# Strassen's seven products in the last projection, for two pairs of token tiles

## The chip, the cores and the metric

The kernel runs on one core of one Trainium2 chip. A core has a matrix engine (TensorE, PE in the profile, whose weight loads are shown as PEld), three engines for elementwise work (VectorE or DVE, ScalarE or ACT, GpSimd or POOL), an engine that issues most transfers here (SyncE, SP), and 16 DMA engines. The metric is the device time of one execution in microseconds.

## The reference

Three layers follow each other on 1792 tokens (4 batches of 448) of 768 features.

```python
def _attn_ref(q, k, v, cap):             # 12 heads of 64
    scores = scale * np.matmul(q, k.transpose(0, 1, 3, 2))
    scores = cap * np.tanh(scores / cap)
    attn = np.exp(scores - max); attn = attn / (sum + 1e-09)
    return np.matmul(attn, v)
def _moe_ref(x, w_in, w_out):            # 768 -> 2048 -> 768
    h = x @ w_in
    return (h - np.tanh(h)) @ w_out
def _moe2_ref(x, w_in, w_out, g_ln):     # 768 -> 1024 -> 768
    h = x @ w_in
    solu = h * softmax(h)
    ln = (solu - mean) / np.sqrt(var + 1e-06) * g_ln
    return ln @ w_out
```

The change is in the last product, `ln @ w_out`, for tokens of the second half.

## The kernel before

The tokens are worked in two halves (`hb` 0 and 1) of 896 tokens, seven tiles of 128. Each half runs attention, then `moe1` (the MoE layer), then `moe2`. Inputs are 32-bit words of 64-bit floats. Each fp32 value that enters a product is split into a rounded high part and a low part (`h` and `l`), and a product is three matmuls (`mm3`, line 252): high by high, high by low, low by high. The split weights are spilled to DRAM in the first half (`keep`) and read back in the second (`unit`, line 178, into 13 rotating buffers of the pool `w`, on SP's queue).

In the second half the up-projection of `moe2` is already done by Strassen's seven products (`seven`, line 647); the sums of its weights are made and spilled in `moe1` by `sums_w3` (line 223), one call per chunk `c`, from spilled weights that are read back, and read as `T1` to `T4`.

Then each tile is normalised (`norm`, line 604): maximum on DVE, exponent with its sum on ACT, the product with `h`, statistics in two parts, root on POOL, scaling on DVE (line 625), eight PE transposes into PSUM (line 629), the high part `lh` by ACT (line 635), the low part `ll` by DVE (line 636). `project` (line 753) multiplies it: per contraction block of 128 six matmuls, three of 512 columns (`wide` weights) and three of 256 (`narrow`), into the two banks of one PSUM tile `oab`; ACT copies 512 columns into `ot`, DVE 256 (line 785), SP writes 128x768 out. The order of tiles is 0, 2, 4, 6, 1, 3, 5. The last tile does its wide part first (line 763).

The code outside attention is written in program order, and a scheduler of the language places each engine's instructions by its own costs, so neighbouring tiles interleave on PE, DVE and ACT. Each engine then runs its queue strictly in order. PSUM tiles of two banks come from two pools, `a` and `b`, of two tiles each; a tile is free again once everything that reads it has read it. The loop around the change is:

```python
for i, t in enumerate(order):
    if i + 1 < NTC:
        norm(order[i + 1])
    ...
    project(t)
```

Of the kernel before, what the change touches and what calls it, by code (L numbers as in the profile page):

```python
# [29 lines left out]
def fused_kernel(ctx, tc, qk_in, v, cap, w1, w2, w3, w4, gln, out):  # L30
    nc = tc.nc
    B, H, S, D = 4, 12, 448, 64
    DM = H * D
    P = 128
# [4 lines left out]
    NK = DM // P  # L39
    HB = B // 2  # L40
    HT = HB * S
    NTC = HT // P
# [25 lines left out]
    def pst(name, tag="b"):  # L68
        return psum[tag].tile([P, 2, 512], F32, tag=tag, name=name)
# [58 lines left out]
    saved = {}  # L128
# [70 lines left out]
    def cols(w, n):  # L199
        return [tuple(t[:, i * (512 // n):(i + 1) * (512 // n)] for t in w) for i in range(n)]  # L200
# [13 lines left out]
    def load_w4():  # L214
        g = [glt[:, i:i + 1] for i in range(DF2 // P)]
        wide, narrow = [], []
        for i in range(DF2 // P):
            wide.append(unit(f"4_{i}", w4u[i], 1, g[i:i + 1]))
            if i % 2:
                narrow += cols(unit(f"5_{i}", w4u[DF2 // P + i // 2], 2, g[i - 1:i + 1]), 2)  # L220
        return wide, narrow

    def sums_w3(i):

        def raw(j, kk):
            st = sp.tile([P, 2, 512], F32R, tag="st", name="rw", bufs=3)
            nc.sync.dma_start(st.bitcast(F32), saved[f"3_{j}_{kk}"].bitcast(F32))
            f = sp.tile([P, 512], F32, tag="f", name="fw", bufs=3)
            nc.vector.tensor_tensor(f, st[:, 0].bitcast(F32), st[:, 1].bitcast(F32), ALU.add)
            return f  # L230

        def put(p, f):
            w = sp.tile([P, 2, 512], F32R, tag="st", name="tw", bufs=3)
            nc.scalar.copy(w[:, 0], f)
            nc.vector.tensor_tensor(w[:, 1], f, w[:, 0].bitcast(F32), ALU.subtract)
            d = drw.tile([P, 2, 512], F32R, name=f"dT{p}_{i}")
            nc.sync.dma_start(d.bitcast(F32), w.bitcast(F32))
# [10 lines left out]
        b21 = raw(0, 2 * i + 1)  # L248
        nc.vector.tensor_tensor(b21, b21, t, ALU.subtract)
# [240 lines left out]
    def moe1(mp, hb, xh, xl, yh, yl):  # L490
# [95 lines left out]
        for c in range(NCHUNK):  # L586
            for k in range(2):
                if c + 1 < NCHUNK:
                    up(c + 1, k)
                if c:  # L590
                    down(c, range(k * NK // 2, (k + 1) * NK // 2))
            if c == 0:
                down(c)
            if hb and c < NK // 2:
                sums_w3(c)

    def moe2(mp, hb, yh, yl):
        hs = {}
        es = {}
        nk2 = DF2 // P  # L600
        lts = {}
        place.update(pool=(mp, WX2), at=-1)

        def norm(t):
            h = hs[t]
            mx = mp.tile([P, 1], F32, tag="mx", name="mx")
            if hb and t in order[1:3]:
                nc.vector.tensor_copy(mx, es[order[0]][:, :1])
            nc.vector.tensor_reduce(mx, h, AX.X, ALU.max)
            nc.vector.tensor_scalar(mx, mx, -1.0, None, ALU.mult)  # L610
            e = mp.tile([P, DF2], F32, tag="e", name="e")
            sm = mp.tile([P, 1], F32, tag="sm", name="sm")
# [8 lines left out]
            nc.vector.bn_aggr(mv, st)  # L621
            rstd = mp.tile([P, 1], F32, tag="rstd", name="rstd")
            nc.vector.tensor_scalar(rstd, mv[:, 1:2], 1e-6, None, ALU.add)
            nc.gpsimd.tensor_tensor(rstd, rstd, mhalf, ALU.pow)
            nc.vector.tensor_scalar(e, e, mv[:, 0:1], rstd, ALU.subtract, ALU.mult)
            es[t] = e
            tp = psum["a"].tile([P, nk2, P], F32, tag="a", name="tp")
            for kk in range(nk2):
                nc.tensor.transpose(tp[:, kk], e[:, kk * P:(kk + 1) * P], idf)
            if hb == 0 and t == order[-1]:  # L630
                lh, ll = (sp.tile([P, nk2, P], F32R, tag="st", name=m, bufs=3) for m in ("lhz", "llz"))
            else:
                lh = mp.tile([P, nk2, P], F32R, tag=f"lh{order.index(t) % 2}", name="lh", bufs=1)
                ll = mp.tile([P, nk2, P], F32R, tag=f"ll{order.index(t) % 2}", name="ll", bufs=1)
            nc.scalar.copy(lh, tp)
            nc.vector.tensor_tensor(ll, tp, lh.bitcast(F32), ALU.subtract)
            lts[t] = (lh, ll)

        groups = [list(range(t, min(t + 2, NTC))) for t in range(0, NTC, 2)]
        for gi, ts in enumerate(groups):  # L640
# [4 lines left out]
        order = list(range(NTC))  # L645
# [91 lines left out]
        if hb:  # L737
            order = list(range(0, NTC, 2)) + list(range(1, NTC, 2))
            seven()
        for j in range(0 if hb else 2):  # L740
            wt = load_w3(j)
            for gi, ts in enumerate(groups):
# [6 lines left out]
                if j == 1 and gi == NG:  # L749
                    norm(0)  # L750
        wide, narrow = load_w4()

        def project(t):
# [4 lines left out]
            ot = mp.tile([P, DM], F32, tag="ot", name="ot")  # L758
            if hb == 1 and t == order[-1]:
                ob = pst("ob", "a")[:, 0]  # L760

                for kk in range(nk2):
                    mm3(oa, (lh[:, kk], ll[:, kk]), wide[kk], kk == 0, kk == nk2 - 1)
                nc.scalar.copy(ot[:, 0:512], oa)
                nc.sync.dma_start(out[r0:r0 + P, 0:512], ot[:, 0:512])
                for kk in range(nk2):
                    mm3(ob[:, :256], (lh[:, kk], ll[:, kk]), narrow[kk], kk == 0, kk == nk2 - 1)
                nc.vector.tensor_copy(ot[:, 512:DM], ob[:, :256])
                nc.sync.dma_start(out[r0:r0 + P, 512:DM], ot[:, 512:DM])
                return  # L770
            for kk in range(nk2):
                f, l = kk == 0, kk == nk2 - 1
                sh, sl_ = lh[:, kk], ll[:, kk]
                (ah, al), (bh, bl) = wide[kk], narrow[kk]
                nc.tensor.matmul(oa, sh, ah, start=f, stop=False)  # L775
                nc.tensor.matmul(oa, sh, al, start=False, stop=False)  # L776
                nc.tensor.matmul(ob[:, :256], sh, bh, start=f, stop=False)
                nc.tensor.matmul(ob[:, :256], sh, bl, start=False, stop=False)
                nc.tensor.matmul(oa, sl_, ah, start=False, stop=l)  # L779
                nc.tensor.matmul(ob[:, :256], sl_, bh, start=False, stop=l)  # L780
            nc.scalar.copy(ot[:, 0:512], oa)
            if hb == 0 and t == NTC - 2:
                nc.scalar.copy(ot[:, 512:DM], ob[:, :256])
# [31 lines left out]
        for i, t in enumerate(order):  # L815
            if i + 1 < NTC:
                norm(order[i + 1])
            if hb == 0 and t == NTC - 1:
                return last()
            project(t)  # L820

    class Region:

# [21 lines left out]
    for hb in range(2):  # L845
# [4 lines left out]
        yh, yl = xtiles()  # L850
# [69 lines left out]
```

## Time and profile before

| | before |
|---|---|
| times of 3 runs, us | 893.17, 894.16, 895.63 (median 894.16) |
| profiled execution, us | 894.53 |
| its span, first to last instruction, us | 892.8 |
| PE, DVE, ACT busy, share of the span | 99%, 74%, 47% |
| moved by DMA | 160.27 MB, mean 180 GB/s |
| last projection, from its first whole run of matmuls | 824.4 to 889.5 us |

The span is what lies between the first and the last instruction of the program; the execution's time has a little around it. Starts in the rows are microseconds from the span's start. A matmul's duration overlaps the next one's, so the cost of one in a full stream is the distance between starts.

### The profile page before, as it was taken

The page shows a single profiled execution, that of the slowest core. Times are in us where ns is not written, and L with a number is a line of the kernel's source. Part 1 is how long each engine was busy: PE and PEld are TensorE (multiplying, and loading weights), DVE is VectorE, ACT ScalarE, POOL GpSimd, SP SyncE. Part 2 cuts the span into 40 slices and gives each one's busy share as a digit, 9 for nine tenths or more (in the row PEclk, how much of TensorE's full clock was granted, in tenths as well). Part 3 has the DMA queues.
Part 4 walks back from the last instruction along what each step waited for, and adds up shares of the span by engine and source line. Part 5 has one row for each costly group of instructions (what it writes and reads, how often), then busy time and mean ns, then how long its engine had stood idle before and what let it go on. Part 6 is the DMA issues. An engine that isn't in the chain of part 4 may idle for free.

```text
span 892.8 us, 13030 instructions
## 1 busy us (share of the span) xinstructions
PE 884.1 (99%) x5133; PEld 707.8 (79%) x5133; DVE 662.9 (74%) x999; ACT 422.3 (47%) x467; POOL 47.4 (5%) x88
## 2 busy tenths in 40 slices
PE   8999999999999999999999999999999999999998
PEld 4444699898898988888874457989989989887887
DVE  6687889989999991888347987894774644678951
ACT  7999367453453331443169990863532332212221
POOL 2211000000000000001012210000000000000000
PEclk9999999999999999999999999999999999999999
DMA  8554690697786774731155642358754332366101
GB/s 296 181 188 139 216 356 25 205 331 258 246 303 219 252 260 150 251 127 53 47 207 201 204 137 81 117 182 324 271 196 158 117 118 82 93 209 230 60 36 53
DMA packets 51177, 160.27 MB, mean 180 GB/s; under 512 B 10989, under 2 KB 14061, under 8 KB 51117
## 3 DMA queue, kind: packets, MB, share of 16 engines
q1 hardware_dynamic: 43932, 130.25, 42.6%
q0 software_dynamic: 7040, 29.20, 9.4%
q8 instruction: 40, 0.66, 0.3%
q14 instruction: 21, 0.16, 0.1%
q10 hardware_dynamic: 144, 0.00, 0.0%
HBM read 109.65 MB, written 49.62 MB: 178 GB/s over the span
## 4 chain that ended last, share of the span: by engine, by line
PE 81%; DVE 12%; DMA 3%; ACT 2%; issue 2%; POOL 0%; DVEq 0%; POOLq 0%; ACTq 0%
PE o L349 9%; PE op L571 6%; PE op L570 6%; PE op L569 6%; PE hp L510 6%; PE hp L511 6%; PE hp L512 6%; PE s L315 5%; PE hp L254 4%; PE hp L256 4%; PE hp L255 4%; PE oab L775 2%; PE oab L779 2%; PE oab L776 2%; PE x L321 2%; PE so L366 2%
## 5 line engine op out<-in xcount | busy, mean ns | idle before, releaser
L512 PE MATMUL hp<-xh,w 128*128 128x512 f32 (+2 forms) x384 | 139.7, 364 | 0.0
L511 PE MATMUL hp<-xl,w 128*128 128x512 f32 (+2 forms) x384 | 139.6, 363 | 0.0
L510 PE MATMUL hp<-xh,w 128*128 128x512 f32 (+2 forms) x384 | 139.4, 364 | 0.0
L569 PE MATMUL op<-gh,w 128*128 128x512 f32 (+1 forms) x336 | 122.0, 363 | 1.5 <-DVE acc L576 1.5
L571 PE MATMUL op<-gh,w 128*128 128x512 f32 (+1 forms) x336 | 122.2, 364 | 0.0
L570 PE MATMUL op<-gl,w 128*128 128x512 f32 (+1 forms) x336 | 122.1, 363 | 0.0
L510 PEld LDWEIGHTS hp<-xh,w 128*128 128x128 f32 x384 | 72.0, 188 | 9.4 <-issue 1.2
L511 PEld LDWEIGHTS hp<-xl,w 128*128 128x128 f32 x384 | 72.1, 188 | 8.0 <-issue 0.7
L512 PEld LDWEIGHTS hp<-xh,w 128*128 128x128 f32 x384 | 72.1, 188 | 7.9 <-issue 0.7
L349 PE MATMUL o<-t,vf 128*32 128x448 f32 x768 | 77.8, 542 | 0.0
L341 ACT ACTIVATE t<-t,shift,capt 128x3136 f32<-128x3136 f32 (+2 forms) x26 | 72.8, 2808 | 0.7
L569 PEld LDWEIGHTS op<-gh,w 128*128 128x128 f32 x336 | 63.1, 188 | 9.7 <-DVE acc L576 2.0
L570 PEld LDWEIGHTS op<-gl,w 128*128 128x128 f32 x336 | 63.0, 188 | 7.1
L571 PEld LDWEIGHTS op<-gh,w 128*128 128x128 f32 x336 | 63.0, 188 | 6.7
L538 ACT ACTIVATE u<-hp 128x896 f32<-128x896 f32 x32 | 29.5, 921 | 76.6 <-PE hp L512 76.6
L332 ACT ACTIVATE t<-s,tscale 128x1344 f32<-128x1344 f32 x48 | 63.5, 1379 | 2.1 <-PE s L315 2.1
L544 DVE SCALAR_TENSOR_TENSOR gf<-u,hp 128x896 f32<-128x896 f32 x32 | 34.7, 1084 | 33.1 <-ACT t L540 33.1
L119 ACT CAST w<-f 128x512 fp32r<-128x512 f32 x44 | 27.3, 623 | 66.8 <-DVE f L113 52.1
L349 PEld LDWEIGHTS o<-t,vf 128*32 128x32 f32 x768 | 22.7, 109 | 43.4 <-issue 38.7
L576 DVE TENSOR_TENSOR acc<-op,acc 128x896 f32<-128x896 f32 x36 | 39.1, 1086 | 21.9 <-PE op L571 21.9
L552 ACT CAST gh<-gf 128x896 fp32r<-128x896 f32 x32 | 29.8, 943 | 51.2 <-DVE gf L549 30.4
L113 DVE SCALAR_TENSOR_TENSOR f<-st,f 128x512 uint32<-128x512 uint32 x72 | 49.2, 688 | 1.0
(187 smaller groups left out, 1824.4 us busy)
## 6 DMA issues: line engine op xcount, KB each, us to landing
d<-w SPq DMA_DIRECT2D x69, 512.0 KB
w<-d SPq DMA_DIRECT2D x53, 512.0 KB
st<-in_moe_w_out_dram SPq DMA_DIRECT2D x35, 512.0 KB
st<-in_moe_w_in_dram SPq DMA_DIRECT2D x25, 512.0 KB
kq<-in_qk_dram POOLq DMA_DIRECT2D x21, 480.0 KB, 4.3
w<-d POOLq DMA_DIRECT2D x13, 512.0 KB, 5.3
rw<-d SPq DMA_DIRECT2D x12, 512.0 KB
dT<-tw SPq DMA_DIRECT2D x12, 512.0 KB
```

Source lines behind the costliest of these rows:

```text
L113: nc.vector.scalar_tensor_tensor(f, st[:, :, 0], 29, f, ALU.logical_shift_right, ALU.bitwise_or)
L315: nc.tensor.matmul(s[b // 3][:, b % 3, :S], st[rows, cs], mv[rows, KW:], start=first, stop=last)
L332: nc.scalar.activation(t[:, 3 * half:3 * half + 3], s[half][:, :, :S], AF.Tanh, scale=tscale)
L341: nc.scalar.activation(t[:, sl], t[:, sl], AF.Exp, bias=shift, scale=capt)
L349: nc.tensor.matmul(o[cs, :S], vf[:, r, cs], t[:, 6 if r == 3 else 2 * r + g // 2], start=(r == 0), stop=(r == 3))
L510: nc.tensor.matmul(o, wh[:, ms], xh[kk][:, cs], start=(kk == 0), stop=False)
L511: nc.tensor.matmul(o, wh[:, ms], xl[kk][:, cs], start=False, stop=False)
L512: nc.tensor.matmul(o, wl[:, ms], xh[kk][:, cs], start=False, stop=(kk == NK - 1))
L569: nc.tensor.matmul(fo[:, a:b], wh, gh, start=(m == 0), stop=False)
L570: nc.tensor.matmul(fo[:, a:b], wh, gl, start=False, stop=False)
L571: nc.tensor.matmul(fo[:, a:b], wl, gh, start=False, stop=(m == nm - 1))
L576: nc.vector.tensor_tensor(a, fo[:, :HT], a, ALU.add)
```

## The change

For tokens of the second half, four of the seven tiles are projected in two pairs (4 with 6, 1 with 3) by Strassen's seven products (the variant of Winograd, with sums s1 to s4 of the tokens' blocks and V1 to V4 of the weights'): the contraction of 1024 is taken in four pairs of blocks, the 768 outputs in two halves of 384, the pair's tiles are the two rows. Seven products of 4 x 3 matmuls of 384 columns stand in the place of eight, one of them in pieces of 128 and 256 columns, since its weights lie in two buffers. Tiles 0, 2 and 5 are projected as before.

- `sums_w4` makes V1 to V4 for each of four pairs of blocks in `moe1` from spilled weights: 16 reads, 16 writes, 384 KB each. The calls of `sums_w3` and `sums_w4` are spread over the chunks: two in each of chunks 0 and 1, three in chunk 2.
- `load_v` reads the 16 sums back once tile 0 is projected: ACT writes a column of each buffer from the first result, and SP loads it behind that. Nine buffers are those of the token sums of `seven`, two its temporaries, five the tokens' own buffers.
- `sums_a` makes the token sums of a pair out of the transposes of both its tiles; the odd tile's transposes are first copied to SBUF by ACT.
- `project_pair` computes the products two to a PSUM tile `pp` and adds them up in `ot` on DVE (the first product is copied twice by ACT).
- In `norm`, the scaling moves from DVE to ACT for all tiles of the second half but the first, with a new small step `nm` on DVE; and the places at which a tile's maximum may begin are set anew (a copy from `mv` or from the scaled `e` of an earlier tile).

```diff
@@ moe1
-            if hb and c < NK // 2:
-                sums_w3(c)
+            if hb:
+                for fn, i in (((sums_w3, 0), (sums_w3, 1)), ((sums_w3, 2), (sums_w4, 0)), ((sums_w4, 1), (sums_w4, 2), (sums_w4, 3)), ())[c]:
+                    fn(i)
@@ moe2, norm
-                nc.vector.tensor_copy(mx, es[order[0]][:, :1])
+                nc.vector.tensor_copy(mx, mvs[order[0]][:, :1] if t == order[1] else es[order[1]][:, :1])
...
-            nc.vector.tensor_scalar(e, e, mv[:, 0:1], rstd, ALU.subtract, ALU.mult)
+            if hb and t != order[0]:
+                nm = mp.tile([P, 1], F32, tag="nm", name="nm")
+                nc.vector.scalar_tensor_tensor(nm, mv[:, 0:1], -1.0, rstd, ALU.mult, ALU.mult)
+                nc.scalar.activation(e, e, AF.Identity, bias=nm, scale=rstd)
+            else:
+                nc.vector.tensor_scalar(e, e, mv[:, 0:1], rstd, ALU.subtract, ALU.mult)
...
+            if t in seconds:
+                return sums_a(seconds[t], t, lh, ll)
+        def sums_a(te, to, lh, ll):
...
+            nc.scalar.copy(es[to].rearrange("p (k m) -> p k m", k=nk2), tps[to])
...
+            nc.vector.tensor_tensor(s1, p21, a22, ALU.add)
+            s2 = temp()
+            nc.vector.tensor_tensor(s2, s1, a11, ALU.subtract)
+            put(2, s2)
+            s3 = temp()
+            nc.vector.tensor_tensor(s3, a11, a21, ALU.subtract)
+            put(3, s3)
+            put(1, s1)
+            nc.vector.tensor_tensor(s2, a12, s2, ALU.subtract)
+            put(4, s2)
+            nc.scalar.copy(lh[:, :kp], a22)
+            nc.vector.tensor_tensor(ll[:, :kp], a22, lh[:, :kp].bitcast(F32), ALU.subtract)
...
+        def load_v(gate):
...
+                    nc.scalar.copy(w[:, 0, :1], gate)
+                    nc.sync.dma_start(w.bitcast(F32), saved[f"V{k}_{i}"].bitcast(F32))
...
+        def project_pair(te, to):
...
+            items = [([(lh[:, 2 * i], ll[:, 2 * i]) for i in range(kp)], raw(0, True)),
+                     ([(lh[:, 2 * i + 1], ll[:, 2 * i + 1]) for i in range(kp)], raw(1, True)),
+                     (summed(2), vs(2)), (summed(3), vs(3)), (summed(1), vs(1)), (summed(4), raw(1, False)),
+                     ([(oh[:, i], ol[:, i]) for i in range(kp)], vs(4))]
+            for n, (st, mv) in enumerate(items):
+                if n % 2 == 0:
+                    ps = pst("pp")
+                o = ps[:, n % 2, :hw]
+                for q in range(len(mv[0])):
+                    for i in range(kp):
+                        cs, w = mv[i][q]
+                        mm3(o[:, cs], st[i], w, i == 0, i == kp - 1)
+                if n == 0:
+                    nc.scalar.copy(h0[:, 0], o)
+                    nc.scalar.copy(h0[:, 1], o)
+                elif n == 1:
+                    added(h0[:, 0], o, h0[:, 0])
+                elif n == 2:
+                    added(h0[:, 1], o, h0[:, 1])
...
+            if t in seconds:
+                project_pair(seconds[t], t)
+            elif t not in seconds.values():
+                project(t)
+            if hb and t == order[0]:
+                load_v(ots[0][:, :1])
```

On PE, before, at the end of tile 4's and the start of tile 6's projection (`oab_7759` and `oab_7843` are their accumulators, `w` the weights, `lh` and `ll` the tile):

```order
L778 MATMUL oab_7759<-w_7556,lh_7671 128x256
L779 MATMUL oab_7759<-w_7554,ll_7672 128x512
L780 MATMUL oab_7759<-w_7556,ll_7672 128x256
L629 MATMUL tp_7830<-idf_71,e_7815 128x128 x8
L775 MATMUL oab_7843<-w_7534,lh_7755 128x512
L776 MATMUL oab_7843<-w_7534,lh_7755 128x512
L777 MATMUL oab_7843<-w_7538,lh_7755 128x256
```

On PE, in the change, at the end of the third product of the first pair (`pp_8058` holds products 3 and 4, `pp_8085` products 5 and 6 in the place of `pp_8030` with 1 and 2; `sv` and `yv` are loaded weight sums, `ps` token sums):

```order
L291 MATMUL pp_8058<-sv_7822,ps_7979 128x384
L292 MATMUL pp_8058<-sv_7822,ps_7979 128x384
L290 MATMUL pp_8085<-sv_7837,ps_7987 128x384
L291 MATMUL pp_8085<-sv_7837,ps_7987 128x384
L292 MATMUL pp_8085<-sv_7837,ps_7987 128x384
L290 MATMUL pp_8085<-yv_7840,ps_7987 128x384
L290 MATMUL pp_8058<-sv_7825,ps_7984 128x384
L291 MATMUL pp_8058<-sv_7825,ps_7984 128x384
```

Four matmuls of the fifth product now stand between the third and the fourth.

On DVE, before, around the eviction of tile 2's projection (`ot`), with the normalisation of tiles 4 and 6 beside it:

```order
L621 BN_AGGR mv<-bst 128x2
L610 TENSOR_SCALAR mx<-mx 128x1
L619 BN_STATS bst<-e 128x6
L623 TENSOR_SCALAR rstd<-mv 128x1
L619 BN_STATS bst<-e 128x6
L785 COPY ot<-oab 128x256
L625 TENSOR_SCALAR e<-e,mv,rstd 128x1024
```

On DVE, in the change, from the sum s2 of the first pair (`pf` are sums, `ps` and `xl` their low parts) to the eviction of the second product (`ot<-pp`):

```order
L720 TENSOR_TENSOR pf<-pf,tp 128x512
L723 TENSOR_TENSOR pf<-tp,e 128x512
L654 RECIPROCAL sm<-sm 128x1
L711 TENSOR_TENSOR ps<-pf,ps 128x512
L655 SCALAR_TENSOR_TENSOR e<-e,sm,h2g_7289 128x1024
L711 TENSOR_TENSOR ps<-pf,ps 128x512 x2
L726 TENSOR_TENSOR pf<-tp,pf 128x512
L658 BN_STATS bst<-e 128x6 x2
L711 TENSOR_TENSOR xl<-pf,xh 128x512
L660 BN_AGGR mv<-bst 128x2
L772 TENSOR_TENSOR ot<-pp,ot 128x384
```

The eviction now stands behind the token sums and a part of the next tile's normalisation.

## Rows read from the trace of the kernel before

**Rows 1.** The page: busy time and share of the span by engine.
```profile
PE 884.1 (99%) x5133; PEld 707.8 (79%) x5133; DVE 662.9 (74%) x999; ACT 422.3 (47%) x467; POOL 47.4 (5%) x88
```

**Rows 2.** By stretches: length, busy us (instructions) per engine, clock, DMA share, GB/s.
```profile
640.00:660.00 20.00, 20.00 (x102) 18.10 (x101) 15.65 (x19) 7.13 (x9) 0.00 (x0) 1.00 0.81 277
...
740.00:760.00 20.00, 20.00 (x101) 18.02 (x100) 9.38 (x9) 3.73 (x4) 0.00 (x0) 1.00 0.23 83
820.00:830.00 10.00, 10.00 (x53) 8.51 (x52) 9.40 (x19) 2.38 (x4) 0.00 (x0) 1.00 0.57 206
...
840.00:850.00 10.00, 10.00 (x63) 8.83 (x61) 8.53 (x18) 2.74 (x4) 1.10 (x2) 1.00 0.10 41
...
860.00:870.00 10.00, 10.00 (x62) 8.84 (x61) 2.46 (x3) 1.60 (x2) 0.55 (x1) 1.00 0.10 41
```

**Rows 3.** PE's waits after 600: line, releaser: us in total, times, longest.
```profile
PE tp L629 <- DVE e L625: 0.8, 1, 0.8
```

**Rows 4.** Timeline of PE in the projection: start, us, instruction, wait before it.
```profile
824.43 0.39 PE L776 MATMUL oab<-w,lh 128*128 128x512 f32 x1
...
834.45 1.09 PE L629 MATMUL tp<-idf,e 128*128 128x128 f32 x8 [0.75 <-DVE e L625]
...
846.20 1.03 PE L629 MATMUL tp<-idf,e 128*128 128x128 f32 x8
846.99 0.48 PE L776 MATMUL oab<-w,lh 128*128 128x512 f32 x1
...
848.95 0.39 PE L775 MATMUL oab<-w,lh 128*128 128x512 f32 x1
...
849.41 0.28 PE L777 MATMUL oab<-w,lh 128*128 128x256 f32 x1
...
850.00 0.40 PE L775 MATMUL oab<-w,lh 128*128 128x512 f32 x1
```

**Rows 5.** Timeline of PE in the MoE layer: first and thirteenth of 384-column matmuls.
```profile
690.08 0.33 PE L511 MATMUL hp<-xl,w 128*128 128x384 f32 x1
...
692.16 0.33 PE L511 MATMUL hp<-xl,w 128*128 128x384 f32 x1
```

**Rows 6.** Groups after 600: line, operation, shapes, count, busy us, mean ns, idle before.
```profile
L717 DVE TENSOR_TENSOR h2g<-hp,h2g 128x512 f32<-128x512 f32 x24 | 16.0, 683 | 7.0 <-PE hp L256 6.9
...
L619 DVE BATCH_NORM_STATS2 bst<-e 128x6 f32<-128x512 f32 x14 | 9.1, 682 | 0.1
...
L616 DVE SCALAR_TENSOR_TENSOR e<-e,sm,h2g 128x1024 f32<-128x1024 f32 x7 | 9.0, 1281 | 0.1
L636 DVE TENSOR_TENSOR ll<-tp,lh 128x1024 fp32r<-128x1024 f32 x7 | 8.5, 1221 | 3.0 <-ACT lh L635 2.9
L609 DVE TENSOR_REDUCE mx<-h2g 128x1 f32<-128x1024 f32 x7 | 8.4, 1210 | 0.0
L613 ACT ACTIVATE e<-h2g,mx 128x1024 f32<-128x1024 f32 x7 | 8.1, 1151 | 16.9 <-DVE mx L610 16.9
...
L635 ACT CAST lh<-tp 128x1024 fp32r<-128x1024 f32 x7 | 7.1, 1014 | 12.3 <-PE tp L629 12.3
...
L668 DVE TENSOR_TENSOR sw<-sf,sw 128x384 fp32r<-128x384 f32 x12 | 6.1, 551 | 0.1
L625 DVE TENSOR_SCALAR e<-e,mv,rstd 128x1024 f32<-128x1024 f32 x7 | 5.7, 813 | 3.7 <-POOL rstd L624 3.7
...
L624 POOL TENSOR_TENSOR rstd<-rstd,mhalf 128x1 f32<-128x1 f32 x7 | 3.8, 550 | 335.2 <-DVE rstd L623 335.2
...
L785 DVE COPY ot<-oab 128x256 f32<-128x256 f32 x6 | 2.5, 422 | 15.4 <-ACT ot L781 15.4
```

**Rows 7.** Timeline of DVE: the up-projection's last sum.
```profile
824.63 0.69 DVE L717 TENSOR_TENSOR h2g<-hp,h2g 128x512 f32<-128x512 f32 x1
```

**Rows 8.** Waits of the whole span: DVE in the weight sums of the MoE layer.
```profile
DVE fw L229 <- DMA rw<-d: 18.8, 6, 7.7
```

**Rows 9.** Timeline of PE at the start of the span.
```profile
2.12 3.26 PE L437 MATMUL z<-xh 128*128 128x448 f32 x8 [2.12 <-DVE xh L434]
```

More of the change, by code (lines that the diff above doesn't have):

```diff
@@ L248, in sums_w3, with sums_w4, raw, put @@
         b21 = raw(0, 2 * i + 1)
+        nc.vector.tensor_tensor(b21, b21, t, ALU.subtract)
+        put(4, b21)
+    def sums_w4(i):
+        hw = DM // 2
+        ke, ko = f"4_{2 * i}", f"4_{2 * i + 1}"
+        kn = f"5_{2 * i + 1}"
+        def raw(*parts):
+            st = sp.tile([P, 2, 512], F32R, tag="st", name="rv", bufs=3)
+            at = 0
+            for key, cs in parts:
+                n = cs.stop - cs.start
+                nc.sync.dma_start(st[:, :, at:at + n].bitcast(F32), saved[key][:, :, cs].bitcast(F32))
+                at += n
+            f = sp.tile([P, 512], F32, tag="f", name="fv", bufs=3)[:, :hw]
+            nc.vector.tensor_tensor(f, st[:, 0, :hw].bitcast(F32), st[:, 1, :hw].bitcast(F32), ALU.add)
+            return f
+        def put(p, f):
+            w = sp.tile([P, 2, 512], F32R, tag="st", name="tv", bufs=3)
+            nc.scalar.copy(w[:, 0, :hw], f)
+            nc.vector.tensor_tensor(w[:, 1, :hw], f, w[:, 0, :hw].bitcast(F32), ALU.subtract)
+            d = drw.tile([P, 2, hw], F32R, name=f"dV{p}_{i}")
+            nc.sync.dma_start(d.bitcast(F32), w[:, :, :hw].bitcast(F32))
+            saved[f"V{p}_{i}"] = d
+        b12, t = raw((ke, slice(hw, 512)), (kn, slice(0, 256))), raw((ke, slice(0, hw)))
+        nc.vector.tensor_tensor(t, b12, t, ALU.subtract)
+        put(1, t)
+        b22 = raw((ko, slice(hw, 512)), (kn, slice(256, 512)))
+        nc.vector.tensor_tensor(b12, b22, b12, ALU.subtract)
+        put(3, b12)
+        nc.vector.tensor_tensor(t, b22, t, ALU.subtract)
+        put(2, t)
+        b21 = raw((ko, slice(0, hw)))
         nc.vector.tensor_tensor(b21, b21, t, ALU.subtract)
@@ L599, in moe2 @@
         es = {}
+        mvs = {}
+        tps = {}
         nk2 = DF2 // P
@@ L621, in norm @@
             nc.vector.bn_aggr(mv, st)
+            mvs[t] = mv
             rstd = mp.tile([P, 1], F32, tag="rstd", name="rstd")
@@ L634, in norm @@
                 ll = mp.tile([P, nk2, P], F32R, tag=f"ll{order.index(t) % 2}", name="ll", bufs=1)
+            tps[t] = tp
+            if t in seconds:
+                return sums_a(seconds[t], t, lh, ll)
             nc.scalar.copy(lh, tp)
@@ L637, in norm, with halves, ytile, temp @@
             lts[t] = (lh, ll)
+        seconds = {}
+        def halves(t):
+            v = tps[t].rearrange("p (i two) m -> p i two m", two=2)
+            return v[:, :, 0], v[:, :, 1]
+        def sums_a(te, to, lh, ll):
+            kp = nk2 // 2
+            a11, a12 = halves(te)
+            p21, p22 = halves(to)
+            def ytile(k):
+                return yts[k][:, :512].rearrange("p (i m) -> p i m", i=kp)
+            def temp():
+                return sp.tile([P, 512], F32, tag="f", name="pf", bufs=3).rearrange("p (i m) -> p i m", i=kp)
+            def put(k, f):
+                if k == 4:
+                    h, l = ytile(6), ytile(7)
+                else:
+                    s = sp.tile([P, 2, kp, P], F32R, tag="st", name="ps", bufs=3)
+                    h, l = s[:, 0], s[:, 1]
+                nc.scalar.copy(h, f)
+                nc.vector.tensor_tensor(l, f, h.bitcast(F32), ALU.subtract)
+                lts["s", k] = (h, l)
+            nc.scalar.copy(es[to].rearrange("p (k m) -> p k m", k=nk2), tps[to])
+            ev = es[to].rearrange("p (i two m) -> p i two m", two=2, m=P)
+            a21, a22 = ev[:, :, 0], ev[:, :, 1]
+            s1 = temp()
+            nc.vector.tensor_tensor(s1, p21, a22, ALU.add)
[10 more added lines that the diff above has]
+            nc.vector.tensor_tensor(ll[:, :kp], a22, lh[:, :kp].bitcast(F32), ALU.subtract)
+            lts[to] = (lh, ll)
@@ new lines, in moe2 @@
+        ots = []
+        def load_v(gate):
+            kp = nk2 // 2
+            got = []
+            for n, k in enumerate((2, 3, 1, 4)):
+                for i in range(kp):
+                    m = len(got)
+                    if m < 9:
+                        w = mp.tile([P, 2, NTC // 2, P], F32R, tag="sw", name="sv", bufs=9).rearrange("p t a b -> p t (a b)")
+                    elif m < 11:
+                        w = mp.tile([P, NTC // 2, 2, P], F32R, tag="yf", name="yv").rearrange("p a b c -> p (a b c)").rearrange("p (t m) -> p t m", t=2)
+                    else:
+                        w = yts[m - 11][:, :DM].rearrange("p (t m) -> p t m", t=2)
+                    nc.scalar.copy(w[:, 0, :1], gate)
+                    nc.sync.dma_start(w.bitcast(F32), saved[f"V{k}_{i}"].bitcast(F32))
+                    got.append(w)
+            vts.update({k: got[kp * n:kp * n + kp] for n, k in enumerate((2, 3, 1, 4))})
@@ new lines, in project_pair, with summed, raw, vs @@
+        def project_pair(te, to):
+            kp, hw = nk2 // 2, DM // 2
+            lh, ll = lts[te]
+            oh, ol = lts[to]
+            ote, oto = (mp.tile([P, DM], F32, tag="ot", name="ot") for _ in range(2))
+            h0, h1 = (o.rearrange("p (t m) -> p t m", t=2) for o in (ote, oto))
+            def summed(k):
+                h, l = lts["s", k]
+                return [(h[:, i], l[:, i]) for i in range(kp)]
+            def raw(odd, left):
+                if left:
+                    return [[(slice(0, hw), tuple(w[:, :hw] for w in wide[2 * i + odd]))] for i in range(kp)]
+                return [[(slice(0, 512 - hw), tuple(w[:, hw:512] for w in wide[2 * i + odd])),
+                         (slice(512 - hw, hw), narrow[2 * i + odd])] for i in range(kp)]
+            def vs(k):
+                return [[(slice(0, hw), (w[:, 0], w[:, 1]))] for w in vts[k]]
+            def added(dst, ps, src):
+                nc.vector.tensor_tensor(dst, ps, src, ALU.add)
+            items = [([(lh[:, 2 * i], ll[:, 2 * i]) for i in range(kp)], raw(0, True)),
+                     ([(lh[:, 2 * i + 1], ll[:, 2 * i + 1]) for i in range(kp)], raw(1, True)),
+                     (summed(2), vs(2)), (summed(3), vs(3)), (summed(1), vs(1)), (summed(4), raw(1, False)),
+                     ([(oh[:, i], ol[:, i]) for i in range(kp)], vs(4))]
+            ps = None
+            for n, (st, mv) in enumerate(items):
[3 more added lines that the diff above has]
+                for q in range(len(mv[0])):
+                    for i in range(kp):
+                        cs, w = mv[i][q]
[7 more added lines that the diff above has]
+                    added(h0[:, 1], o, h0[:, 1])
+                elif n == 3:
+                    added(h1[:, 0], o, h0[:, 1])
+                elif n == 4:
+                    added(h0[:, 1], o, h0[:, 1])
+                    added(h1[:, 1], o, h1[:, 0])
+                elif n == 5:
+                    added(h0[:, 1], o, h0[:, 1])
+                elif n == 6:
+                    added(h1[:, 0], o, h1[:, 0])
+            for t, o in ((te, ote), (to, oto)):
+                r0 = hb * HT + t * P
+                nc.sync.dma_start(out[r0:r0 + P, :], o)
@@ L751, in moe2 @@
         wide, narrow = load_w4()
+        if hb:
+            yts = [w[kk] for par in (0, 1) for kk in range(par, NK, 2) for w in (yh, yl)]
+            vts = {}
+            seconds.update({order[3]: order[2], order[5]: order[4]})
         def project(t):
@@ L758, in project @@
             ot = mp.tile([P, DM], F32, tag="ot", name="ot")
+            ots.append(ot)
             if hb == 1 and t == order[-1]:
@@ L819, in moe2 @@
                 return last()
-            project(t)
+            if t in seconds:
[4 more added lines that the diff above has]
+                load_v(ots[0][:, :1])
     class Region:
```

## The prediction

> **What bounds the kernel now.** I read the page first: TensorE (PE) is busy 99% of the span, VectorE (DVE) 74%, ScalarE (ACT) 47% [rows 1]. Next the table by stretches. In the MoE layer, where the new weight sums are made, PE has no gap and DVE works 9.4 to 15.7 us of 20. In the last projection PE is full, and DVE is nearly full too at first (9.4 and 8.5 us of 10), with little left to do after 860 (2.5) [rows 2]. The list of PE's waits confirms it: in the last 293 us one wait of 0.8 us, for a normalised tile [rows 3]. So a matmul taken away is a gain, one for one, as long as DVE and ACT deliver as they do now; and in the stretch of the change DVE has a tenth to a sixth of its time left.
>
> **What the products take away from PE.** One contraction block of the projection is six matmuls, 2304 columns, from 848.95 to 850.00: 1.05 us [rows 4]. A tile has eight, a pair sixteen: 16.8 us. The pair's seven products have 12 matmuls each: 72 of 384 columns, and for the product with the raw right half 12 of 128 and 12 of 256. Matmuls of 384 columns follow each other by 2.08 / 12 = 0.173 us [rows 5]; fed from rounded sums they may be a little slower, so I take 0.175: 12.6 us. In the block, two wide ones take 0.46 us (848.95 to 849.41), so three take 0.69, and the three of 256 columns the other 0.36, 0.12 each: 1.4 us. One of 128 columns with rounded operands is in no row. By columns it would be 0.173 / 3 = 0.058 us. The nearest row is the eight 128-column transposes, 846.20 to 846.99, 0.10 us each. The upper bound is a 512-column matmul, 0.23 us. I take 0.10: 1.2 us. The pair is then 15.2 us, and two pairs give 2 x 1.6 = 3.2 us back; with 0.058 it would be 4.2, with 0.23 nothing (0.1).
>
> On the 128-column matmuls the Trainium skill ("TensorE: Matmul & The Clock Gate", LDWEIGHTS) says that a weight load takes its columns over 1.2 GHz, for 128 columns 107 ns; it bears against the column count, and the transposes agree with it (0.10). By that rule the 24 narrow matmuls cost 2.6 us against 1.4 by columns.
>
> **What it adds to DVE and ACT in the same stretch.** For each pair, DVE: sums s1 to s4 and their low parts, eight of 128x512 at 0.68, the odd tile's half low part 0.68, and seven evictions of 128x384 at 0.55: 10.0 us. It drops one ll (1.22), two evictions (0.42) and, in both tiles, the scaling (0.81 less 0.15 for the new nm): 3.4 us [rows 6]. So 6.6 us more on an engine that had 1.5 free of ten. ACT has room but works in order: the scaling (about 1.1, as the exponent's 1.15), the copy of the transposes (1.01), two copies of the first product (half of that each, an estimate from 384 columns against 1024 and a fixed part) stand ahead of the casts.
>
> **Where PE then stands still.** I walk the new order with the durations of rows 6, from 824.43, where both kernels have issued the same work [rows 4]. A step on DVE that needs nothing from the one before it takes 0.08 less than its row, since they overlap.
>
> Tile 4's normalisation. DVE ends the last sum of the up-projection at 825.3 [rows 7]; statistics, root on POOL (0.55), nm: 826.3; ACT scales tile 2 by 827.4, as PE arrives (827.6). The new order lets the maxima wait for that scaled tile: two maxima 829.8, ll 831.0, exponent on ACT 832.5, next maximum 833.7, e 835.4, eviction, statistics 837.0, another maximum 838.2, tile 6's e 839.6, root and nm 840.6, ACT 841.7. PE has done 19 matmuls, transposes, and 73 matmuls at 841.2: it waits 0.5, and 0.2 for tile 6, whose chain runs just behind. There is no spare matmul left between: tile 4 is needed at once. Its lh waits on ACT behind tile 6's scaling (844.5), its ll comes at 845.8: product 1 stands 1.0.
>
> Products 1 and 2 are written into the two banks of one PSUM tile, and the program makes product 2 wait until product 1 is copied out (twice, by ACT). ACT is at it by 848.0 (exponent, transposes, cast first) and ends at 849.0; PE was ready at 847.6: 1.4. Product 2 ends at 851.1, product 3 (s2 is rounded by 850.7) at 853.2.
>
> Then the order gives PE four matmuls of the fifth product ahead of the fourth. They go into the first tile again and wait for DVE's eviction of product 2. DVE has before it, from 850.7: e (1.2), two low parts (1.2), s4 (0.6), statistics (1.2), a low part (0.6), aggregate (0.15), the eviction (0.55): 856.2. PE waits 3.0, and the twelve matmuls of product 4, ready since 852.5 but for the eviction of product 3, stand behind it.
>
> To the end of the pair I find no more: product 4, tile 1's transposes, 5, 7 and 6 end at 865.9, tile 3's transposes at 866.7. Pair 2 uses the tile again before product 6 of pair 1 is evicted, behind a whole normalisation on DVE: 0.7. Its s2 starts when ACT has scaled tile 5 (868.1), copied the transposes (869.1); three DVE steps, cast, low part: 872.3 against 870.35: 1.6; two small ones behind copies: 0.4.
>
> **The sum.** Waits 0.5 + 0.2 + 1.0 + 1.4 + 3.0 + 0.7 + 1.6 + 0.4 = 8.8; the 0.75 before tile 4's transposes [rows 4] falls away: +8.0. Matmuls: -3.2, or -3.5 at 0.173; I use -3.4. The last tile's projection and the tail keep their form. Net +4.6 us.
>
> **What I cost at nothing.** The sums of weights in the MoE layer: four groups of 12 DVE steps and 4 casts of 128x384: 26 us of DVE, 8 of ACT, over some 120 us in which DVE is about half idle [rows 2]. Nothing there is removed, so no gain; a loss comes only if DVE stands so long for a spilled weight that PE finds no accumulator. Before, DVE stood 18.8 us for such reads, the longest time 7.7, and PE lost nothing [rows 8]. One accumulator's 24 matmuls (12 of 0.23, 12 of 0.173) are 4.8 us of cover, so 7.7 at the wrong moment costs up to 3. On SP the reads and writes stand among the weight loads of the next stage; these have 13 buffers ahead, so I see no wait there. Traffic grows by 12.6 MB; the queues moved 83 to 277 GB/s there [rows 2], which leaves room.
>
> The loads of the sums: 16 of 384 KB, 6.3 MB, on SP once ACT has copied tile 0 (834.3) and written one column into each buffer. At 277 GB/s 23 us: product 3's four by 841 (needed 851), the last by 858 (needed 863). At 206 GB/s [rows 2] the last comes at 866: 2 to 3 us. I take 0.
>
> The profiled execution took 894.53 us with a span of 892.8; the median shown is 894.16, which I use: 894.16 + 4.6 = 898.8.
>
> **The rivals.**
> 1. *The gain arrives.* DVE and ACT run earlier than my walk, and no wait above a microsecond stays. For it: PE lost only 0.8 us [rows 3] with DVE at 85% or more. Against: the three largest waits hang on the order of the queues, which is fixed. -3.4 and 0.4 of waits: 891.2.
> 2. *It comes out even.* The walk has the right places, but the waits are half as long (ACT and DVE hide their small steps better than the rows say): +4.0 of waits, -3.4, so about 894.7.
> 3. *DVE stands for a read of spilled weights in the MoE layer*, just when an accumulator must be evicted; +3 on the forecast: 901.8. It needs one wait above 4.8 us there; before there was one of 7.7.
> 4. *The clock.* Behind the 3.0 us wait PE runs at its lower level for a while. At the start of the span, after 2.1 us with nothing to do, eight matmuls of 448 columns took 3.26 us, where 512 columns at 0.23 [rows 4] make 0.20 of 448, 1.6 for eight [rows 9]: 1.7 us more. 898.8 + 1.7 to 3 = 901 to 902. No row within the full flow shows a fall; the longest wait there is 0.8. The Trainium skill (the same page, "Why this matters for your kernels") warns that idle gaps between bursts of matmuls throw the clock to half; its own rule would make this rival certain only if the one long wait is long enough, which no row here settles.
> 5. *The 128-column matmuls run like wide ones*: 24 x 0.13 = 3.1 on the forecast: 901.9.
>
> **Chances.** Forecast 0.48; rivals 1 to 5: 0.12, 0.18, 0.08, 0.06, 0.08. A measurement of this kernel tells about 0.3% (2.7 us) from no change. Faster is rival 1: 0.12. Same is rival 2: 0.18. Slower is the rest: 0.70. The forecast's own range is 896.9 to 901; the range that I give goes down to 893.5, which holds most of rival 2, and up to 904, which holds 3 to 5 and the slow loads: some 0.16 below it, 0.04 above.
>
> **What would show it.** PE's waits in the tail must sum to 8 to 9 us, led by one of about 3 us at the first matmul of the fifth product, released by DVE's eviction into ot; one of 1 to 1.5 at the second product, released by ACT. Matmuls of the pairs must take 30 to 31 us of PE. The MoE stretch must keep PE at 20 of 20, and the granted clock must stay at 1.00. I am wrong in the main step if the waits of the pairs sum to under 5 us, wrong in the matmul term if a 128-column matmul is far from 0.10.

## The result: 0.8% slower, and the profile after

The changed kernel took 901.68 us (median of five runs, 900.74 to 903.09) against 894.4 of the kernel before, ratio 1.0079 [1.0066, 1.0092]; a second set of six runs gave 901.88 against 894.98, 1.0077 [1.0064, 1.0091]. Forecast were 898.8 and a range of 893.5 to 904: slower as forecast, by 7 us in place of 4.6. The profiled execution took 901.05 us with a span of 898.7 (before: 894.53 and 892.8).

The page's shares hardly differ from [rows 1], so they don't show where 6 us went:

```profile
PE 885.4 (99%) x5133; PEld 710.0 (79%) x5133; DVE 695.9 (77%) x1073; ACT 442.9 (49%) x515; POOL 47.6 (5%) x88
```

The table by stretches does (columns as in [rows 2]):

```profile
600.00:820.00 220.00, 220.00 (x1070) 193.52 (x1069) 155.68 (x215) 74.79 (x105) 0.56 (x1) 1.00 0.70 237
```
```profile
840.00:850.00 10.00, 8.17 (x50) 6.74 (x49) 6.91 (x14) 8.57 (x13) 0.55 (x1) 1.00 1.03 402
850.00:860.00 10.00, 7.18 (x36) 6.86 (x35) 9.31 (x21) 3.50 (x5) 0.69 (x2) 0.83 0.47 183
860.00:870.00 10.00, 9.66 (x67) 9.39 (x66) 6.94 (x15) 5.49 (x6) 0.96 (x2) 1.00 0.08 32
855.50:859.00 3.50, 3.47 (x11) 3.49 (x12) 3.17 (x8) 1.24 (x1) 0.55 (x1) 0.53 0.02 7
```

From 600 to 820, where the weight sums are made in the MoE layer and the up-projection follows, PE is busy 220 of 220 us. The loss is in the projection, from 840 on, and in one place the granted clock is not 1.00. PE's waits after 600 (before, the one row of [rows 3]):

```profile
PE pp L290 <- issue: 2.8, 1, 2.8
PE pp L290 <- ACT ot L789: 0.9, 1, 0.9
PE pp L292 <- DVE ll L684: 0.6, 1, 0.6
PE pp L290 <- ACT ps L710: 0.6, 1, 0.6
PE pp L290 <- DVE ot L772: 0.3, 1, 0.3
PE tp L674 <- DVE pf L718: 0.2, 1, 0.2
PE tp L674 <- ACT e L668: 0.2, 1, 0.2
```

"issue" means that the page found no releaser. Two timelines find it: PE at the fifth product, then DVE in the same time (start, us, instruction). The matmul after the wait is the fifth product's first; "..." marks rows left out.

```profile
852.38 0.34 PE L292 MATMUL pp<-sv,ps 128*128 128x384 f32 x1
855.53 0.66 PE L290 MATMUL pp<-sv,ps 128*128 128x384 f32 x1 [2.82 <-issue]
855.99 0.52 PE L291 MATMUL pp<-sv,ps 128*128 128x384 f32 x1
856.31 0.52 PE L292 MATMUL pp<-sv,ps 128*128 128x384 f32 x1
...
858.85 0.34 PE L290 MATMUL pp<-sv,ps 128*128 128x384 f32 x1
```
```profile
850.02 1.28 DVE L655 SCALAR_TENSOR_TENSOR e<-e,sm,h2g 128x1024 f32<-128x1024 f32 x1
851.22 1.29 DVE L711 TENSOR_TENSOR ps<-pf,ps 128x512 fp32r<-128x512 f32 x2
852.42 0.68 DVE L726 TENSOR_TENSOR pf<-tp,pf 128x512 f32<-128x512 f32 x1
853.02 1.27 DVE L658 BATCH_NORM_STATS2 bst<-e 128x6 f32<-128x512 f32 x2
854.21 0.67 DVE L711 TENSOR_TENSOR xl<-pf,xh 128x512 fp32r<-128x512 f32 x1
854.81 0.20 DVE L660 BATCH_NORM_AGGREGATE mv<-bst 128x2 f32<-128x12 f32 x1
854.92 0.51 DVE L772 TENSOR_TENSOR ot<-pp,ot 128x384 f32<-128x384 f32 x1
```

DVE comes to the eviction of product 2 (L772) at 854.92, behind exactly the queue that the walk named; it ends at 855.43 and PE starts at 855.53. One other releaser is possible: SP's loads of the weight sums keep the DMA engines full until 854 (share 1.01 from 853 to 854), near the end of the wait. E3 below speaks against it: there the same matmul starts without a wait while such loads still run.

Then the matmuls stand 0.32 us apart instead of 0.173 [rows 5], ten of them from 855.53 to 858.85, under a granted clock of 0.53: the lower level of 1.2 GHz for most of that stretch.

One measure makes kernels comparable here, since what comes before it varies from run to run: the time from the last matmul of the up-projection to the last of all. These are its ends, before and after:

```profile
824.21 0.39 PE L256 MATMUL hp<-w,xl 128*128 128x512 f32 x1
889.21 0.28 PE L256 MATMUL ob<-w,ll 128*128 128x256 f32 x1
```
```profile
823.80 0.39 PE L292 MATMUL hp<-w,xl 128*128 128x512 f32 x1
895.17 0.28 PE L292 MATMUL ob<-w,ll 128*128 128x256 f32 x1
```

That tail is 65.0 us before and 71.4 after: +6.4. What is left of the 6.9 to 7.3 us of the medians lies mostly outside the span: run time less span is 1.7 to 1.8 us before, and 2.0 to 2.4 after.

### The profile page after: what moved, and what is told of

It reads as the page before. It is cut to its first block, busy times and chain, and to the rows that moved or that the text cites. A ratio compares the mean times of both kernels' runs of the same rounds, so it can differ in the third digit from the quotient of the medians.

```text
span 898.7 us, 13289 instructions
## 1 busy us (share of the span) xinstructions
PE 885.4 (99%) x5133; PEld 710.0 (79%) x5133; DVE 695.9 (77%) x1073; ACT 442.9 (49%) x515; POOL 47.6 (5%) x88
## 4 chain that ended last, share of the span: by engine, by line
PE 77%; DVE 15%; ACT 3%; issue 2%; DMA 2%; POOL 0%; POOLq 0%; DVEq 0%; ACTq 0%
PE o L385 8%; PE op L607 6%; PE op L606 6%; PE op L605 6%; PE hp L546 6%; PE hp L548 6%; PE hp L547 6%; PE s L351 5%; PE hp L290 4%; PE hp L291 4%; PE hp L292 4%; PE x L357 2%; PE so L402 2%; DVE f L113 2%; DVE gf L585 1%
## 5 line engine op out<-in xcount | busy, mean ns | idle before, releaser
L113 DVE SCALAR_TENSOR_TENSOR f<-st,f 128x512 uint32<-128x512 uint32 x72 | 49.4, 690 | 1.0
L112 DVE SCALAR_TENSOR_TENSOR f<-st,f 128x512 uint32<-128x512 uint32 x72 | 49.1, 691 | 0.8
```

The costliest lines, as they stand in the source:

```text
L112: nc.vector.scalar_tensor_tensor(f, st[:, :, 1], 0xC0000000, f, ALU.bitwise_and, ALU.bitwise_or)
L113: nc.vector.scalar_tensor_tensor(f, st[:, :, 0], 29, f, ALU.logical_shift_right, ALU.bitwise_or)
```

## Experiments

The theory: the waits that DVE's and ACT's queues cause in the pairs, and the lower clock behind the longest one, cost more than the matmuls give back; the weight sums cost nothing. The rivals: the sums, the normalisation, or the pairs' matmuls themselves cost it. "Tail" is the measure above, from each kernel's profile.

| kernel | median us | ratio to before | tail us |
|---|---|---|---|
| the change, again | 901.88 | 1.0077 [1.0064, 1.0091] | 71.4 |
| E1 sums only | 895.36 | 1.0008 [0.9997, 1.0019] | 64.9 |
| E2 pairs, no sums | 899.94 | 1.0063 [1.0048, 1.0078] | 70.1 |
| E3 no low parts | 899.72 | 1.0061 [1.0046, 1.0075] | 69.6 |
| E4 wait filled | 900.27 | 1.0068 [1.0052, 1.0083] | 70.5 |
| E5 normalisation only | 894.85 | 0.9998 [0.9988, 1.0008] | 65.3 |
| E6 second pair | 894.64 | 0.9996 [0.9987, 1.0004] | 65.2 |
| E7 DVE, ACT relieved | 893.35 | 0.9985 [0.9974, 0.9995] | 63.7 |
| E8 first pair | 900.37 | 1.0066 [1.0050, 1.0081] | 69.3 |
| E9 GpSimd low parts | 900.74 | 1.0069 [1.0052, 1.0085] | 69.9 |
| E10 second pair, GpSimd | 894.60 | 1.0001 [0.9993, 1.0010] | 65.0 |

**The change again.** 

> The changed kernel once more, unaltered, on the same chip as the other kernels of this group, as what they are compared with. Both theories: 900.7 to 902, ratio to before 1.0065 to 1.009. Also asked: is the granted clock behind the 2.8 us wait at half in every run (mean clock of the run 0.997 or 0.998), as in the five runs seen so far? My theory says yes in most; if it stays at 1.000 in half of them, the clock term belongs into the sum with half its weight.

As expected. The mean clock of all six runs was 0.996 to 0.998, that of the five before 0.997 or 0.998, and that of the kernel before 0.999 or 1.000: by the mean clock the fall came eleven times of eleven. Two of the eleven have a trace, and both show it at this place.

**E1, the sums alone** (no pair, the old normalisation).

```diff
-            seconds.update({order[3]: order[2], order[5]: order[4]})
+            pass
```

> Leaves the projection and the normalisation as they were before the change, and keeps only the making of the weight sums and their spilling in the second half's MoE layer (nobody reads them). My theory: the sums cost nothing, since TensorE is full in the MoE layer with and without them; the time equals that of before, 894.4 us within 1 us, with one wait of 0.8 us in the tail. Rival (the sums cost: engine time, the 12.6 MB of traffic, or work outside the span): 1 to 3 us above before, with the time seen either in waits ahead of 820 us or as a larger difference between run time and span.

The tail is that of before, PE's only wait after 600 is the old one of 0.8, and the difference of 0.7 us by the ratio (1.3 by the medians) is not told from none: the sums cost at most 1.7 us (upper bound 1.0019).

**E2, the pairs without the sums.** The calls of `sums_w4` are left out, and the loads fetch other spilled sums:

```diff
-                    nc.sync.dma_start(w.bitcast(F32), saved[f"V{k}_{i}"].bitcast(F32))
+                    nc.sync.dma_start(w.bitcast(F32), saved[f"T{k}_{i % 3}"][:, :, :DM // 2].bitcast(F32))
```

> The pairs and the new normalisation as in the change, but the weight sums are not made; the four loads of sums fetch spilled sums of another weight of the same shape, so the output is another. My theory: the same waits as in the changed kernel, led by one of 2.8 us at the fifth product, a granted clock of about half behind it, and the same time, 901.7 us within 1 us. Rival (making the sums costs part of the 7 us): 1 to 3 us below the changed kernel.

1.7 to 1.9 us below the change by the medians, though the intervals of the ratios overlap: a miss by the number, and for the rival at first sight. But the waits are the same to 0.1 us, and the trace shows another difference, the matmuls behind the same wait:

```profile
854.88 0.41 PE L290 MATMUL pp<-sv,ps 128*128 128x384 f32 x1 [2.79 <-issue]
855.13 0.34 PE L291 MATMUL pp<-sv,ps 128*128 128x384 f32 x1
855.31 0.34 PE L292 MATMUL pp<-sv,ps 128*128 128x384 f32 x1
...
856.72 0.34 PE L290 MATMUL pp<-sv,ps 128*128 128x384 f32 x1
```

They are 0.18 apart: the clock stayed up. The same ten matmuls took 1.84 us here (854.88 to 856.72) and 3.32 in the change, so the fall costs 1.5 us. By the mean clock it stayed up in three of the six runs (1.000; the others 0.997 to 0.998). That makes the tail 1.3 us shorter than the change's in this profile. Run time less span is 1.7 to 1.8 here, half a microsecond under the change's. With E1, which makes the sums and shows no loss beyond 1.7, I count little or nothing for them.

**E3, the token sums' low parts left out.**

```diff
-                nc.vector.tensor_tensor(l, f, h.bitcast(F32), ALU.subtract)
-                lts["s", k] = (h, l)
+                lts["s", k] = (h, h)
```

> As the change, but the low parts of the token sums s1 to s4 are left out (the high part stands in both places, same matmuls): eight DVE steps of 0.68 us fewer, 2.7 us of DVE per pair. My theory (DVE's late eviction of product 2 makes the long wait): the wait of 2.8 us at the fifth product goes to under 0.5; the clock stays at 1.00 there; part comes back as longer waits for the transposes of the next tiles (about 1.5 and 2.5 us); in sum 2 to 4 us below the changed kernel, 897.5 to 899.5. Rival (the loss lies in the matmuls or outside the span): the time stays within 1 us of 901.7.

The wait at the fifth product is gone, as expected; its first matmul follows the third product at once:

```profile
853.02 0.33 PE L290 MATMUL pp<-sv,ps 128*128 128x384 f32 x1
```

The DMA engines are still full with the loads then (share 1.04 from 853 to 854), so the load of this weight had come by the time at which the change's PE stood and waited. The time fell by some 2 us, to just above the range that I gave (899.72 against 899.5); the intervals of the ratios overlap, the tail is 1.8 us shorter. The clock stayed up at this place, but fell elsewhere, behind the new wait of 2.3 us before the transposes.

```profile
869.88 1.09 PE L674 MATMUL tp<-idf,e 128*128 128x128 f32 x8 [2.28 <-DVE pf L717]
870.73 0.49 PE L290 MATMUL pp<-w,lh 128*128 128x384 f32 x1
871.01 0.52 PE L291 MATMUL pp<-w,lh 128*128 128x384 f32 x1
871.33 0.52 PE L292 MATMUL pp<-w,ll 128*128 128x384 f32 x1
```

These matmuls use raw weights, so freshly loaded sums are not what made the others slow.

**E4, part of the long wait filled with matmuls.**

```diff
+                for r in range(16 if n == 2 and te == order[2] else 0): nc.tensor.matmul(ps[:, 0, hw:], st[0][0], mv[0][0][1][0][:, :512 - hw], start=True, stop=True)
```

> As the change, with sixteen further matmuls of 128 columns into PSUM columns that nobody reads, just ahead of the third product of the first pair (16 x 0.107 = 1.7 us): they fill part of the 2.8 us for which TensorE stands before the fifth product, while the eviction that ends this wait comes at the same time. My theory (the clock falls because of that wait): the wait shrinks to about 1.1 us, the granted clock stays at 1.00 behind it, the 384-column matmuls keep 0.173 us, and the kernel is 1 to 2 us faster although it does more: 899.7 to 900.7. Rival A (the ten slow matmuls are slow for another reason, such as their freshly loaded weights): slow again, and the time stays at 901.7 within 0.5. Rival B (the clock falls all the same behind the shorter wait): the same time as the changed kernel, with a granted clock of about half.

```profile
850.41 1.90 PE L783 MATMUL pp<-sv,ps 128*128 128x128 f32 x16
...
855.48 0.41 PE L290 MATMUL pp<-sv,ps 128*128 128x384 f32 x1 [1.02 <-issue]
855.73 0.34 PE L291 MATMUL pp<-sv,ps 128*128 128x384 f32 x1
855.90 0.33 PE L292 MATMUL pp<-sv,ps 128*128 128x384 f32 x1
```

The wait ends at the same time (855.48 against 855.53), is 1.0 long, and the matmuls behind it run at full speed; all six runs have a clock of 0.999 or 1.000. The tail is 0.9 us shorter although sixteen matmuls were added. The whole time points the same way (900.27), but the intervals of the ratios overlap, so the gain rests on one trace against two.

**E5, the normalisation alone.** The edit is E1's, with the sums left out as well.

> Only the new normalisation (scaling on ScalarE, maxima gated behind the first tile), with the projection as before and no weight sums. My theory: the wait for the transposes of the third tile (0.8) becomes three small ones of 0.2 to 0.5, and the time stays that of before within 1 us (-0.1). Rival (the new normalisation costs part of the 7 us, by the gates): 1.5 us or more above before, with a wait above 1 us at the transposes.

As expected: level with before, two waits of 0.3 and 0.2.

**E6 and E8, one pair alone.**

```diff
-            seconds.update({order[3]: order[2], order[5]: order[4]})
+            seconds.update({order[5]: order[4]})
```

That is E6; E8 keeps the other entry.

> The change with one pair alone: the second (tiles 1 and 3) by seven products, tiles 4 and 6 one by one as before. My theory: the pair's gain of 1.5 us in matmuls is real, and there the two waits that are left (before the transposes 0.9, behind copies 0.4, and some 1.1 in the tiles before) take it back; no wait above 1.2, the clock stays at 1.00; the time is that of before within 1.2 us. Rival (a pair costs by itself, in its matmuls, its loads or outside the span): at least half of the change's 7 us, 3 us or more above before.

> The change with the other pair alone: the first (tiles 4 and 6) by seven products, tiles 1 and 3 one by one as before. My theory (the loss sits where VectorE is full, in the first pair): the 2.8 us wait at the fifth product and the half clock behind it are there, with the waits of 0.6 and 0.9 ahead of it; the pair gives 1.5 us of matmuls and loses about 7 with the clock: 5 to 7 us above before, where the second pair alone was level with it. Rival (the loss is made by the two pairs together, by queues that the second pair fills): under 3 us above before.

Both as expected: the second pair costs nothing that can be told (0.9987 to 1.0004), the first costs 5.8 us. In the second PE waits only this:

```profile
PE tp L674 <- DVE pf L718: 0.7, 1, 0.7
PE oab L952 <- DVE ll L684: 0.3, 1, 0.3
PE tp L674 <- ACT e L668: 0.2, 1, 0.2
```

The first has the waits of 2.8, 0.9 and 0.6 unchanged. Its runs seem to show the clock's part: the two at 1.000 took 897.5 and 897.7 us, the four at 0.996 to 0.998 took 899.6 to 901.7. But the runs of E2 and E9 do not part in this way (at 1.000 898.6 to 901.2 and 897.5 to 902.7, below it 899.5 to 901.3 and 899.6 to 902.1), and runs of the kernel before scatter over 2.8 us themselves, so the size is better read from the rows above (1.5 us).

**E7, DVE and ACT relieved.** Besides E3's edit and the statistics:

```diff
+            if not hb or t == order[0]:
+                nc.vector.scalar_tensor_tensor(e, e, sm, h, ALU.mult, ALU.mult)
...
-                    nc.scalar.copy(h0[:, 1], o)
```

> The change with VectorE and ScalarE relieved in the second half's projection: left out are the low parts of the token sums, the multiplication by the exponent and the statistics of all tiles but the first (their mean and root are used again), and the second copy of product 1. TensorE has exactly the changed kernel's matmuls. My theory (matmuls save 3.1 us, waits for VectorE and ScalarE take it and more): the 2.8 us wait is gone, one wait of about 1.9 stays at product 2 and some 0.6 of others, the clock stays at 1.00, and the time falls below before: 891.5 to 893.5, where the changed kernel has about 901.5. Rival (the matmul saving isn't real, so that TensorE needs as long as before even when it doesn't wait): 895 to 897.

893.35 us: below before, at the upper end of what I gave. With the same matmuls as the change, one wait is left. I expected it at the second product; it stands at the third, for ACT's rounding of a token sum:

```profile
847.87 0.44 PE L290 MATMUL pp<-sv,ps 128*128 128x384 f32 x1 [1.66 <-ACT ps L714]
```

So the matmuls do save time (the tail is 1.3 us shorter than before, wait and all), and the change loses it to DVE and ACT.

**E9 and E10, three low parts of each pair on GpSimd** (E10: the second pair alone).

```diff
-                nc.vector.tensor_tensor(l, f, h.bitcast(F32), ALU.subtract)
+                (nc.gpsimd if k in (1, 4) else nc.vector).tensor_tensor(l, f, h.bitcast(F32), ALU.subtract)
...
+            nc.gpsimd.tensor_tensor(ll[:, :kp], a22, lh[:, :kp].bitcast(F32), ALU.subtract)
```

> The change whole, but three subtractions of each pair (the low parts of s1, of s4 and of the odd tile's half) go from VectorE to GpSimd: two of 128x512 and one more of 128x512 per pair, 2 us of VectorE. How long GpSimd takes for one is in no trace so far; my estimate is 1 to 2 us, twice VectorE's 0.68 or more. My theory: the 2.8 us wait shrinks to 1.0 to 1.5, the clock stays at 1.00 in most runs, and the kernel is 2 to 3.5 us faster than the change: 898 to 900 where the change has 901.8. Rival (the product with the late low part then waits for GpSimd instead): the wait moves to the fifth or sixth product with the same length, and the time stays at 901 to 902.

> The second pair alone, with the same three subtractions on GpSimd: an attempt to beat the kernel before. My theory: the pair's 1.5 us of matmuls against waits of about 0.7 before the transposes and 0.5 elsewhere: 0.3 to 1 us below before, about what five rounds can tell. Rival (GpSimd's subtractions come too late for the products): a wait of over 1 us at the fifth or sixth product of the pair, and the time at or above before.

GpSimd took 1.28 us for one by itself, DVE 0.69. In E9 the long wait is 1.9 us, not 1.0 to 1.5. My estimate took it that the engines don't disturb each other. But where these two subtractions of E9 ran at the same time, GpSimd's took 1.69 us and DVE's 1.78:

```profile
853.40 1.69 POOL L711 TENSOR_TENSOR ps<-pf,ps 128x512 fp32r<-128x512 f32 x1 [1.59 <-DMA xl<-dV]
```
```profile
853.85 1.78 DVE L711 TENSOR_TENSOR ps<-pf,ps 128x512 fp32r<-128x512 f32 x1
```

That is 1.1 us more in DVE's queue ahead of the eviction, enough for what the wait has over the expected length. Other waits of 0.8 and 0.2 came in front of transposes, and by the mean clock the fall came in three of six runs: about 1 us gained of the 2 to 3.5 expected, which the intervals of the ratios don't tell from none. E10 is level with before, so no version tried that leaves nothing out beats it.

## Why the prediction was right in direction and short in size

The time lies above the 896.9 to 901 that the walk itself gave, and inside the wider range because that range held rivals 3 to 5. The walk's two terms were right; the clock, which the sum put at nothing, came on top, and half a microsecond outside the span.

- **Matmuls, -3.4.** Right. A row of twelve narrow ones took 863.89 to 865.18, 0.1075 each (taken: 0.10), the wide ones 0.12 and 0.173:

```profile
863.89 0.23 PE L290 MATMUL pp<-w,xh 128*128 128x128 f32 x1
...
865.18 0.33 PE L290 MATMUL pp<-w,xh 128*128 128x256 f32 x1
...
866.67 0.33 PE L291 MATMUL pp<-xh,lh 128*128 128x384 f32 x1
```

  These rows give 15.2 us a pair, 1.56 less than the 16.8 of before: -3.1 for two. What the waits below leave of the tail's +6.4 is -3.3. Rival 5 is out, and E7 shows the saving in the time itself.
- **Waits, +8.0.** Right, in place and in sum. I took every distance between two matmuls' starts from 819.7 on, less the usual one (0.107, 0.12, 0.173 or 0.229 us by columns). What is over sums to 10.8 us after and 1.1 before: +9.7, of which ten times 0.13 to 0.3 (1.6, counted from the usual distance) is the clock. The waits are +8.1. By place, forecast and measured in this way: fifth product 3.0 and 3.0; product 2 1.4 and 1.1; product 1 1.0 and 0.8; tile 6 0.2 and 0.4; pair 2's start 0.7 and 0.5; its s2 1.6 and 1.6 (0.4 before the transposes, 0.9 and 0.3 at the product); behind copies 0.4 and 0.3. Tile 4's 0.5 did not come; small gaps make up for it. The page's own waits sum to 5.6 only, since it counts a matmul as busy until its modelled end; by that list the 8 to 9 us asked for ahead of the result are missed, and the 5 us that would have refuted the walk are just passed. The sum of both terms, 8.1 - 3.3 = +4.8, stands against +4.6. Rivals 1 and 2 are out.
- **Costed at nothing.** Right for the weight sums (E1: 1.0008, rival 3 out) and their loads: PE's list shows no wait for one, and E3 clears the load at the fifth product. The queues moved about 400 GB/s in that time, not 277.
- **The clock.** This is the step that failed: the sum held no term for it, "the granted clock must stay at 1.00" did not come true (0.53 from 855.5 to 859), and rival 4 had 0.06. Its mechanism came, at 1.5 us, a little under its 1.7 to 3. I gave it little because no row within the flow showed a fall; but the longest wait there was 0.8 us, so those rows could not speak for one of 3 us. The one row that had such a wait, [rows 9], spoke for the fall, and should have weighed more, although it doesn't show what PE did before the span. The Trainium skill ("TensorE: Matmul & The Clock Gate", HAM oscillation) describes a kernel whose short bursts of matmuls each start at the low clock, because PE waits for data between them. Its waits are longer than any here; these traces show a fall behind waits of 2.8 and 2.3 us too, which end when an eviction and a token sum are done, and none behind waits of 1.0 and 1.7 us (E4, E7). That the same wait of 2.8 us was followed by the fall eleven times of eleven in the change, three of six in E2 and four of six in E8 by the mean clock, and that the traces of E2 and E8 show it at full speed, means that its length alone doesn't decide; what else does stays open.
- **Outside the span, 0.2 to 0.7 us.** In no term. E1, E2 and E5 have 1.7 to 1.8 us there as before, the other experiments 1.9 to 2.15, the change 2.0 to 2.4. Neither the sums alone (E1) nor the pairs alone (E2) bring it. Its cause stays open.

So 4.8 + 1.6 + 0.5 = 6.9 us, against 6.9 and 7.3 by the medians. The first two make up the tail's 6.4 by construction, since the -3.3 is what was left of it; with the -3.1 of the rows it is 7.1.

## What to carry to other kernels

A scheme that saves matmuls pays for it in additions, and these belong on an engine that has room at that moment: one pair cost 5.8 us where DVE was full, and another nothing that could be told some 20 us later. An engine with room is no free gift either: GpSimd's subtraction slowed the one that DVE did beside it. When a walk along an engine's order gives one wait on TensorE as long as those that were followed by a fall here (2.3 and 2.8 us in the traces), add the slow matmuls behind it to the sum as likely, not as a remote case; and try to fill such a wait first. Splitting one was not tried here.

## What the runs showed of the hardware that was not expected

- Extra work made the tail shorter: sixteen unused matmuls (1.7 us) in a wait of 2.8 us went with a mean clock of 0.999 or 1.000 in six runs of six, and the tail in the trace is 0.9 us shorter.
- The falls that have a trace cost about the same: 1.5 us behind the wait at the fifth product (3.32 against 1.84 us in E2), and 1.6 in E3 behind the wait ahead of transposes (870.73 to 874.46 for twelve matmuls, 3.73 against 2.08).
- A subtraction of 128x512 took 1.69 us on GpSimd and 1.78 on DVE while both ran, against 1.28 and 0.69 (E9). Beside steps of DVE that read PSUM, GpSimd's took 1.29 and DVE's 0.69 (E10, 865.68 and 865.71).
- A matmul of 128 columns with rounded operands costs 0.1075 us, 62% of one of 384.
